# Loading q and k of the third batch in row order, turning two head pairs by TensorE and two by DMA, with the steps ordered anew

## The chip, the cores and the metric

The kernel runs on one core of one Trainium2 chip. The metric is the device time of one execution in microseconds (us). Most executions of one kernel agree within about 1%; an execution whose time is over 1.5% above the fastest of the same kernel is called slow here and is left out of comparisons. The medians quoted are those of all runs of a kernel, the ratios those of its fast runs. The profile of a kernel is one execution; its span (first to last instruction) is 1.7 us shorter than the time of the same execution.

## The reference, cut to what matters

```python
# q, k, v: [4 batches, 8 heads, 768, 64] f32;  window 128, 4 sink tokens
scores = (q @ k.T) / sqrt(64)               # keep: 0 <= i - j < 128, or j < 4
a      = softmax(where(keep, scores, -1e9))
x      = (a @ v) as [4, 768, 512]           # heads side by side
# ---- gated block
h      = gelu_tanh(x @ w_in)                # [4, 768, 1024]
u, v_  = h[..., :512], h[..., 512:]
v_n    = (v_ - mean) / sqrt(var + 1e-6) * g_ln
v_s    = einsum('ts,bsd->btd', w_sg, v_n) + b_sg      # mixes the 768 positions: "spatial"
out    = x + (u * v_s) @ w_out
```

## The kernel before

The kernel is one list of steps, run in the order written. `NAME.b.p` is a step on batch b; each engine takes its own instructions from the list in order. The steps that the argument needs:

- `LQ`, `LK`, `LV`: loads of q, k, v, issued by GpSimd; they are cast to bf16 on the way.
- `TQ`/`TK`, then `EQ`/`EK`: transposes of a head pair on TensorE, and the copy out of PSUM (by ScalarE `A` or VectorE `D`). Where a DMA turns the pair, there is only `EQ`/`EK`, issued by SyncE.
- `KS`, `SK`: the four sink keys of all head pairs of a batch, and their scores. `QK`, `EX`, `MK`, `AV`: scores, exponent, mask (`D` VectorE, `P` GpSimd), product with v.
- `RS`: 1/sigma, a power on GpSimd. `NM`, `Z`: negated mean over sigma, and the normalised v. `SP`: the spatial matmuls. `GT`, `GM`: gate. `OU`, `RA`, `ST`: output matmuls, residual, store. `WT`, `WE`: transposes of w_sg and their copies. `HM.n`: n dummy matmuls.

```python
STEPS = """
... XT.0.3 VSM.1 MV.0.0 XE.0.3.A LV.1.3 VSM.3 VSM.2 MV.0.1 GV.0.0 LG WT.2
... BN.0.2 RS.0.1 WT.4 GU.0.1 TQ.1.1
TQ.1.0 EQ.1.1.A MU.0.2 LQ.2.0 WE.4 EQ.1.0.A NM.0.1 RS.0.2 WE.0 Z.0.3.A ...
... EQ.2.0.D SP.0.0.1 EX.1.3.0 LK.2.0 ...
"""                                     # cut: 655 steps in all
DT = (3,)                               # batches whose q and k are turned by DMA
# ...
qn  = Ring("qn", 4, [128, NT, 2, Dh], BF16)      # row order, one head pair each
kn  = Ring("kn", 4, [128, NT, 2, Dh], BF16)
q16 = Ring("q16", 2, [128, 4, NT, Dh], BF16)     # four heads each
# ...
def load(ring, src, b, i):              # one DMA for four heads, 1536 bytes in a row
    n = 2 if b == 0 else 4
    hs = slice(n * i, n * i + n)
    dst = ring.get((b, n * i // 4))[:, n * i % 4:n * i % 4 + n].rearrange("p h t d -> p h (t d)")
    return nc.gpsimd.dma_start(out=dst, in_=src[b, hs].rearrange("h (p t) d -> p h (t d)", p=128))

def rows(ring, src, b, p):              # row order: one DMA for each head, 256 bytes in a row
    t = ring.new((b, p))
    return [nc.gpsimd.dma_start(out=t[:, :, hl, :], in_=src[b, 2 * p + hl].rearrange("(t p) d -> p t d", p=128))
            for hl in range(2)][-1]

def LQ(b, i):
    if (b, i) == (0, 0):
        return first("q", q)
    return rows(qn, q, b, i) if b in DT else load(q16, q, b, i)
# ...
def transposes(name, ring, b, p):       # 12 transposes of half width
    # ...
    for t in range(NT):
        for hl in range(2):
            nc.tensor.transpose(ps[64 * hl:64 * hl + 64, t, :], src[:, 2 * (p % 2) + hl, t, :], iden)

def turned(dst, name, src, b, p, e):
    if b in DT:
        return nc.sync.dma_start_transpose(out=dst.new((b, p))..., in_=src[b, p]...)
    copy(e, ...)                        # PSUM to SBUF
# ...
def RS(b, jj):
    r = rs[b][:, part(jj)]
    nc.gpsimd.tensor_tensor(r, r, neg_half[:, part(jj)], op=ALU.pow)
```

The softmax here doesn't subtract the row's maximum and nothing guards it: scores larger than these inputs give would overflow.

Of the kernel before, what the change touches and what calls it, by code (L numbers as in the profile page):

```python
# [16 lines left out]
ZERO IDEN LQ.0.0 LK.0.0 LQ.0.1 FILL LK.0.1 LC MASK VSK LV.0.0 MASK0 CQ.0.0.D LQ.0.2 HM.7 TQ.0.0 CK.0.0.D EQ.0.0.A  # L17
LK.0.2 TK.0.0 LV.0.1 EK.0.0.A TQ.0.1 QK.0.0.2 KS.0.0 LQ.0.3 EQ.0.1.D QK.0.0.1 EX.0.0.2 SK.0.0 LK.0.3 VSM.0 TK.0.1
LV.0.2 EK.0.1.D SX.0.0 QK.0.0.0 MK.0.0.2.P EX.0.0.1 HM.1 TQ.0.2 KS.0.1 LV.0.3 EX.0.0.0 QK.0.1.2 EQ.0.2.D SK.0.1
MK.0.0.1.P TK.0.2 EX.0.1.2 QK.0.1.1 EK.0.2.D SX.0.1 QK.0.1.0 LW.0 AV.0.0.1 EX.0.1.1 MK.0.0.0 LW.1 KS.0.2 EX.0.1.0 HM.1  # L20
AV.0.0.0 NR.0.0.1 QK.0.2.2 SK.0.2 MK.0.1.1.P NR.0.0.0 EX.0.2.2 TQ.0.3 TK.0.3 SX.0.2 QK.0.2.1 LWS MK.0.1.0 EQ.0.3.A
QK.0.2.0 EK.0.3.D AV.0.1.0 EX.0.2.1 MK.0.2.2.P NR.0.1.0 EX.0.2.0 LWO QK.0.3.1 MK.0.2.1.D XT.0.0 EX.0.3.1 KS.0.3 LQ.1.0
QK.0.3.0 MK.0.2.0 SK.0.3 AV.0.2.1 XE.0.0.A LK.1.0 MK.0.1.2.D AV.0.2.0 NR.0.2.1 SX.0.3 MK.0.3.1.P QK.0.3.2 AV.0.1.1
EX.0.3.0 NR.0.2.0 LV.1.0 NR.0.1.1 EX.0.3.2 MK.0.3.0 LV.1.1 HM.4 XT.0.2 MK.0.3.2.D XE.0.2.A AV.0.3.0 LQ.1.1 AV.0.3.1
NR.0.3.0 LK.1.1 NR.0.3.1 XT.0.1 LV.1.2 XE.0.1.D XT.0.3 VSM.1 MV.0.0 XE.0.3.A LV.1.3 VSM.3 VSM.2 MV.0.1 GV.0.0 LG WT.2
WT.3 WE.2 WT.5 GV.0.1 MV.0.2 WE.3 BN.0.0 MU.0.0 GV.0.2 WE.5 BN.0.1 WT.0 GU.0.0 MU.0.1 BN.0.2 RS.0.1 WT.4 GU.0.1 TQ.1.1
TQ.1.0 EQ.1.1.A MU.0.2 LQ.2.0 WE.4 EQ.1.0.A NM.0.1 RS.0.2 WE.0 Z.0.3.A MU.0.3 Z.0.0.D Z.0.1.A NM.0.2 Z.0.4.D Z.0.2.A
TK.1.0 Z.0.5.D WT.1 GU.0.3 EK.1.0.D SP.0.1.0 GU.0.2 WE.1 SP.0.1.2 GT.0.1.0 GM.0.1.0.P QK.1.0.1 GT.0.1.2 QK.1.0.0
TQ.1.2 EX.1.0.1 GM.0.1.2.D TQ.1.3 EQ.1.2.D SP.0.1.3 SP.0.0.2 GT.0.1.3 EQ.1.3.A MK.1.0.1.D TK.1.3 EX.1.0.0 GM.0.1.3.D
TK.1.2 GT.0.0.2 QK.1.0.2 EK.1.2.A SP.0.1.1 EK.1.3.D GM.0.0.2.P EX.1.0.2 QK.1.2.2 MK.1.0.0 SP.0.0.3 EX.1.2.2 MK.1.0.2.D  # L30
GT.0.1.1 QK.1.2.0 QK.1.3.0 GT.0.0.3 EX.1.2.0 TQ.2.0 GM.0.1.1.P TK.1.1 EQ.2.0.D SP.0.0.1 EX.1.3.0 LK.2.0 MK.1.2.0
LV.2.0 EK.1.1.A QK.1.2.1 GM.0.0.3.D QK.1.3.2 OU.0.5 EX.1.2.1 GT.0.0.1 LV.2.1 KS.1.0 OU.0.3 EX.1.3.2 RA.0.5 MK.1.2.1.P
SK.1.0 RA.0.3 ST.0.5 QK.1.3.1 SX.1.0 LQ.2.1 QK.1.1.2 MK.1.3.2.D TQ.2.1 ST.0.3 AV.1.0.1 MK.1.3.0 LK.2.1 EQ.2.1.A
AV.1.0.0 MK.1.2.2.D LV.2.2 AV.1.2.0 NR.1.0.1 EX.1.3.1 AV.1.2.1 NR.1.0.0 GM.0.0.1.P TK.2.1 EX.1.1.2 QK.1.1.0 NR.1.2.1
TK.2.0 MK.1.3.1.P EK.2.1.A QK.1.1.1 NR.1.2.0 EX.1.1.0 LV.2.3 MK.1.1.2.D AV.1.3.1 EX.1.1.1 MK.1.1.0 QK.2.1.2 LQ.3.0
AV.1.3.0 NR.1.3.1 EX.2.1.2 OU.0.4 NR.1.3.0 EK.2.0.A MK.1.1.1.P QK.2.1.1 RA.0.4 QK.2.1.0 EX.2.1.1 XT.1.3 LK.3.0 XT.1.1
ST.0.4 XE.1.3.D AV.1.1.0 EX.2.1.0 TQ.2.3 XE.1.1.D AV.1.1.1 NR.1.1.0 LV.3.0 EQ.2.3.A QK.2.0.2 MK.2.1.0 QK.2.0.1 TQ.2.2
EX.2.0.2 LQ.3.1 NR.1.1.1 TK.2.3 EQ.2.2.A TK.2.2 EK.2.3.D XT.1.2 EK.2.2.A LK.3.1 XT.1.0 XE.1.2.D QK.2.0.0 EX.2.0.1
SP.0.0.0 KS.2.0 LV.3.1 EX.2.0.0 XE.1.0.D SK.2.0 GT.0.0.0 MV.1.0 LQ.3.2 SX.2.0 MK.2.0.0 GM.0.0.0.D EQ.3.0 MK.2.0.1.D
OU.0.1 MK.2.0.2.P GV.1.0 AV.2.0.0 RA.0.1 MK.2.1.2.P MV.1.1 MK.2.1.1.P ST.0.1 EK.3.0 BN.1.0 MV.1.2 GV.1.1 BN.1.1  # L40
# [12 lines left out]
QK.3.3.1 AV.3.0.1 NR.3.1.1 AV.3.0.0 Z.2.5.D NR.3.0.1 SP.2.0.1 EX.3.3.1 MK.3.3.2.D QK.3.2.2 NR.3.0.0 MK.3.3.1.P
QK.3.2.1 SP.2.0.3 EX.3.2.2 GT.2.0.1 EX.3.2.1 MK.3.2.2.P AV.3.3.1 GT.2.0.3 QK.3.2.0 NR.3.3.1 MK.3.2.1.P SP.2.0.0
EX.3.2.0 GM.2.0.3.P AV.3.2.1 GT.2.0.0 QK.3.3.0 GM.2.0.1.P NR.3.2.1 SP.2.1.3 EX.3.3.0 XD.3.1 GM.2.0.0.D SP.2.0.2
MK.3.2.0 GT.2.1.3 AV.3.2.0 MK.3.3.0 SP.2.1.2 GM.2.1.3.P GT.2.0.2 AV.3.3.0 NR.3.2.0 SP.2.1.1 GM.2.0.2.P NR.3.3.0
SP.2.1.0 GT.2.1.2 XD.3.0 GT.2.1.1 GM.2.1.2.P OU.2.1 GT.2.1.0 GM.2.1.1.P MV.3.2 RA.2.1 GM.2.1.0.P OU.2.3 GV.3.2 ST.2.1
OU.2.2 RA.2.3 OU.2.4 ST.2.3 RA.2.2 MV.3.0 BN.3.2 ST.2.2 MV.3.1 RA.2.4 RS.3.2 GV.3.0 ST.2.4 NM.3.2 BN.3.0 Z.3.5.A
MU.3.0 GV.3.1 Z.3.4.A OU.2.0 BN.3.1 GU.3.0 MU.3.2 RA.2.0 RS.3.1 MU.3.1 GU.3.2 ST.2.0 NM.3.1 OU.2.5 Z.3.0.A Z.3.3.D
Z.3.1.D Z.3.2.A MU.3.3 RA.2.5 GU.3.1 ST.2.5 SP.3.1.1 GU.3.3 SP.3.0.1 GT.3.1.1 GM.3.1.1.P SP.3.0.3 GT.3.0.1 GM.3.0.1.D  # L60
SP.3.1.0 GT.3.0.3 GM.3.0.3.D SP.3.0.2 GT.3.1.0 GM.3.1.0.P SP.3.0.0 GT.3.0.2 GM.3.0.2.D SP.3.1.3 GT.3.0.0 GM.3.0.0.P
SP.3.1.2 GT.3.1.3 GM.3.1.3.P OU.3.1 GT.3.1.2 OU.3.0 GM.3.1.2.D RA.3.1 OU.3.3 RA.3.0 ST.3.1 OU.3.4 ST.3.0 RA.3.3 OU.3.5
ST.3.3 OU.3.2 RA.3.5 RA.3.2 ST.3.5 ST.3.2 RA.3.4 ST.3.4
"""



HOLDS = "LG<LWS"


DT = (3,)


@with_exitstack
def kernel(
# [127 lines left out]
    def LQ(b, i):  # L203
        if (b, i) == (0, 0):
            return first("q", q)
# [96 lines left out]
    def TQ(b, p):  # L302
        transposes("q", q16, b, p)
# [269 lines left out]
```

## Time and profile before

| | before |
|---|---|
| time, median of 3 runs | 164.76 us (163.81 to 166.53, the last one slow) |
| span, mean granted clock | 160.9 us, 0.998 |
| TensorE busy | 147.7 us (92%) |
| GpSimd busy | 88.9 us (55%) |
| first spatial matmul of batch 1, 2, 3, 4 | 39.87, 84.22, 116.02, 143.14 us |

How to read the profile lines: PE is TensorE, PEld its weight loads, DVE VectorE, ACT ScalarE, POOL GpSimd, SP SyncE. L457 is line 457 of that kernel; x6 counts instructions that stand together; `a<-b` is what is written and what is read; a bracket is the idle time of the engine just before, and what ended it. After is a longer file, so the lines have other numbers there and in the experiments: 1/sigma L457 becomes L474, the spatial matmuls L499 become L528, the output matmuls L516 become L544, the half-width transposes L300 become L305, the row loads L199, the loads of v L214 become L217.

The last row of the table is the ruler. TensorE runs the spatial matmuls of each batch at one fixed place in its own order, so the starts of the four groups cut the span into stretches. (The new order moves a few of TensorE's steps from one stretch to the next, so differences of a few tenths mean nothing.) The starts are read from TensorE's timeline (the chain of waits, from which the prediction took 40.03, counts the first of them 0.16 us later). From start to end the five stretches of before are 39.87, 44.35, 31.80, 27.12 and 17.8 us.

### The profile page before, as it was taken

The numbers are of one execution on the slowest core, as the hardware profiler recorded it, in microseconds if no ns is written. First come the engines' busy times: TensorE is split into PE (matmuls) and PEld (weight loads), VectorE is DVE, ScalarE is ACT, GpSimd is POOL, SyncE is SP. The second block draws the span as 40 slices with busy tenths as digits, with TensorE's granted clock in tenths as the row PEclk, the third lists the DMA queues.
The fourth block names the chain that finished last, engine by engine and source line by source line (L and its number), as shares of the span: only waits on it lengthen the run. The fifth ranks groups of instructions, "written<-read, shape, count | busy, mean of one in ns | idle before, by whom it ended". The sixth has DMA issues, their size and how long they took to land.

```text
span 160.9 us, 3798 instructions
## 1 busy us (share of the span) xinstructions
PE 147.7 (92%) x1508; PEld 86.6 (54%) x1521; DVE 132.0 (82%) x305; ACT 100.4 (62%) x117; POOL 88.9 (55%) x119
## 2 busy tenths in 40 slices
PE   4958798999999979999999999999999999999980
PEld 1436465576655657644565664545756644555530
DVE  4579999599899998977999999789978848857761
ACT  3379985569968789985378678545886025770000
POOL 7999993433226999997994860004076721204400
PEclk9999999999999999999999999999999999999999
DMA  4999999999990999999999955710302545030055
GB/s 162 174 163 175 199 213 206 204 212 176 178 116 5 145 251 183 194 155 145 214 235 164 123 121 108 230 65 9 125 0 48 94 124 195 0 132 0 4 198 195
DMA packets 63122, 22.70 MB, mean 141 GB/s; under 512 B 51456, under 2 KB 59904, under 8 KB 63104
## 3 DMA queue, kind: packets, MB, share of 16 engines
q0 software_dynamic: 45600, 11.80, 75.1%
q1 hardware_dynamic: 17504, 10.66, 26.5%
q8 instruction: 12, 0.20, 0.5%
q14 instruction: 6, 0.05, 0.1%
HBM read 24.81 MB, written 6.29 MB: 193 GB/s over the span
## 4 chain that ended last, share of the span: by engine, by line
PE 64%; POOL 17%; DVE 8%; DMA 3%; ACT 3%; issue 2%; DVEq 0%; POOLq 0%
PE mm L499 18%; PE sc L478 13%; PE mm L516 10%; PE sc L436 10%; POOL v_sb L214 5%; PE sc L350 4%; DMA q<-in_q_dram 3%; DVE x_sb L410 3%; POOL qn L196 3%; PE mm L300 3%; DVE P L365 2%; POOL P L369 2%; POOL kn L196 2%; PE mm L390 2%; ACT P L358 2%
## 5 line engine op out<-in xcount | busy, mean ns | idle before, releaser
L358 ACT ACTIVATE P<-sc 128x1024 bf16<-128x1024 f32 (+1 forms) x48 | 43.9, 962 | 7.0 <-PE sc L350 6.5
L499 PE MATMUL mm<-wsgT,z 128*128 128x384 bf16 x192 | 34.4, 327 | 0.0
L509 POOL TENSOR_TENSOR wsg_gated<-gtmp,uT 128x384 bf16<-128x384 bf16 x19 | 17.9, 951 | 22.9 <-DVE gtmp L504 19.5
L499 PEld LDWEIGHTS <-z 128*128 128x128 bf16 x192 | 17.5, 98 | 12.1 <-issue 1.8
L504 DVE SCALAR_TENSOR_TENSOR gtmp<-mm,g_sb,b_bc 128x384 bf16<-128x384 f32 x32 | 19.4, 614 | 5.6 <-PE mm L499 5.5
L440 ACT ACTIVATE vt<-sc 128x1024 f32<-128x1024 f32 x12 | 12.3, 1024 | 17.0 <-PE sc L436 17.0
L478 PE MATMUL sc<-xT,w_in_sb 128*128 128x384 bf16 x128 | 22.4, 326 | 0.1
L516 PE MATMUL mm<-w_out_sb,wsg_gated 128*128 128x512 bf16 x88 | 21.6, 379 | 0.5 <-issue 0.2
L436 PE MATMUL sc<-w_in_sb,xT 128*128 128x512 bf16 x94 | 21.9, 379 | 0.1
L520 DVE TENSOR_TENSOR ot<-mm,x_sb 128x512 f32<-128x512 f32 x24 | 16.2, 689 | 6.3 <-PE mm L516 6.2
L457 POOL TENSOR_TENSOR rs<-rs,neg_half 128x4 f32<-128x4 f32 (+1 forms) x8 | 7.1, 886 | 25.7 <-DVE rs L452 24.9
L365 DVE TENSOR_TENSOR P<-P,mask 128x1024 bf16<-128x1024 bf16 (+1 forms) x32 | 21.1, 685 | 0.0
L214 POOL DMA_DIRECT2D v_sb<-in_v_dram x16 | 16.9, 1059 | 5.3 <-DMA wsg_gated<-in_moe_w_sg_dram 4.1
L410 DVE TENSOR_TENSOR x_sb<-mm,rcp 128x384 bf16<-128x384 f32 x32 | 17.8, 558 | 1.1
L390 PE MATMUL mm<-v_sb,P 128*128 128x65 bf16 x192 | 17.0, 194 | 1.6 <-DVE P L365 0.9
L484 ACT ACTIVATE uT<-sc 128x768 bf16<-128x768 f32 x16 | 12.8, 807 | 8.1 <-PE sc L478 8.1
L449 DVE BATCH_NORM_STATS2 st<-vt 128x6 f32<-128x512 f32 x24 | 16.2, 675 | 1.5 <-ACT vt L440 1.5
L478 PEld LDWEIGHTS <-w_in_sb 128*128 128x128 bf16 x128 | 12.4, 98 | 9.0
L390 PEld LDWEIGHTS <-P 128*128 128x128 bf16 x192 | 14.5, 98 | 4.7 <-DVE P L365 1.6
L396 PE MATMUL mm<-v_sb,P 128*128 128x65 bf16 x160 | 15.7, 194 | 0.6 <-POOL P L373 0.4
L350 PE MATMUL sc<-qT,kT 64*128 64x256 bf16 x192 | 15.5, 264 | 0.7 <-DVE kT L221 0.3
L436 PEld LDWEIGHTS <-xT 128*128 128x128 bf16 x96 | 9.2, 98 | 10.5 <-issue 0.2
(73 smaller groups left out, 227.4 us busy)
## 6 DMA issues: line engine op xcount, KB each, us to landing
out_dram<-ot SPq DMA_DIRECT2D x24, 256.0 KB, 2.3
v_sb<-in_v_dram POOLq DMA_DIRECT2D x16, 192.0 KB, 7.9
q<-in_q_dram POOLq DMA_DIRECT2D x4, 384.0 KB, 13.7
k<-in_k_dram POOLq DMA_DIRECT2D x4, 384.0 KB, 13.1
wsg_gated<-in_moe_w_sg_dram POOLq DMA_DIRECT2D x1, 1152.0 KB, 12.3
w_in_sb<-in_moe_w_in_dram POOLq DMA_DIRECT2D x2, 512.0 KB, 7.6
qn<-in_q_dram POOLq DMA_DIRECT2D x8, 96.0 KB, 7.2
kn<-in_k_dram POOLq DMA_DIRECT2D x8, 96.0 KB, 6.0
```

Source lines behind the costliest of these rows:

```text
L214: return nc.gpsimd.dma_start(out=v_sb[b % len(v_sb)][:, 2 * p:2 * p + 2, :, 0:Dh].rearrange("p h t d -> p (h t) d"), in_=v[b, 2 * p:2 * p ...
L350: nc.tensor.matmul(sc[:, hl, 256 * jl:256 * jl + n], kT[b, p][rows, 128 * j:128 * (j + 1)], qT[b, p][rows, 128 * j:128 * j + n], start=Tru ...
L358: nc.scalar.activation(out=pt[:, :, 0:w], in_=sc_ring[b, p, g][:, :, 0:w], func=AF.Exp, scale=scale)
L365: nc.vector.tensor_mul(pt[:, :, 0:w], pt[:, :, 0:w], m.unsqueeze(1).to_broadcast([128, 2, w]))
L390: nc.tensor.matmul(av[:, il, hl, :], P[b, p, i // 2][:, hl, 256 * (i % 2):256 * (i % 2) + 128], vb[:, h, i, :], start=first, stop=False)
L410: nc.vector.tensor_mul(xs[:, 3 * half:3 * half + 3, 128 * p:128 * (p + 1)].rearrange("p t (h d) -> p t h d", h=2), av[:, :, :, 0:Dh], rcp. ...
L436: nc.tensor.matmul(hp[:, jl, :], xT[b][:, j, c, :], w_in_sb[:, c, d_half:2 * d_half], start=(c == 0), stop=(c == KD - 1))
L478: nc.tensor.matmul(hp[:, n, 0:NH], w_in_sb[:, c, 128 * dc:128 * (dc + 1)], xT[b][:, 3 * hf:3 * hf + 3, c, :], start=(c == 0), stop=(c == K ...
L499: nc.tensor.matmul(ps[:, 0:NH], z[b][:, si, 128 * dc:128 * (dc + 1)], wsgT[:, si, NH * hf:NH * (hf + 1)], start=(si == 0), stop=(si == NT ...
L504: nc.vector.scalar_tensor_tensor(out=gtmp.new((b, hf, dc)), in0=mm_ring["g", b, hf, dc][:, 0:NH], scalar=g_sb[:, dc:dc + 1], in1=b_bc[:, N ...
L509: (nc.vector if e == "D" else nc.gpsimd).tensor_mul(gatedT[:, (2 * b + hf) % 3, dc, :], gtmp[b, hf, dc], uT[b][:, dc, NH * hf:NH * (hf + 1)])
L516: nc.tensor.matmul(ps, gatedT[:, (2 * b + hf) % 3, dc, 128 * tl:128 * (tl + 1)], w_out_sb[:, dc, :], start=(dc == 0), stop=(dc == KU - 1))
```

## The change

Its intent: q and k of the third batch come in row order, as those of the fourth do already. Then two of the four head pairs need no TensorE transpose (a DMA turns them), and the other two are turned in full width, 6 transposes in place of 12. The third batch gets buffers of its own at once, so that its loads no longer wait for transposes of the first two. The last output tiles leave partly in halves, and the whole list of steps is ordered anew.

```diff
-DT = (3,)
+TURN = ('SSSS', 'SSSS', 'RRDD', 'DDDD')      # per batch and head pair: S half width, R rows and TensorE, D rows and DMA
+LAST = (5,)                                  # output tiles of the last batch that leave in halves

 def LQ(b, p):
     ...
-    return rows(qn, q, b, i) if b in DT else load(q16, q, b, i)
+    return load(q16, q, b, p) if TURN[b][p] == "S" else rows(qn, q, b, p)      # LK the same

 def transposes(name, s, r, b, p):
     for t in range(NT):
+        if TURN[b][p] == "R":
+            nc.tensor.transpose(ps[:, t, :], r[b, p][:, t, :, :].rearrange("p h d -> p (h d)"), iden)
+            continue
         for hl in range(2): ...

 def turned(dst, name, src, b, p, e):
-    if b in DT:
+    if TURN[b][p] == "D":
         return nc.sync.dma_start_transpose(...)
+    if TURN[b][p] == "R":
+        return copy(e, ...)                   # contiguous
...                                           # cut: OU, RA, ST in halves (OB, RB, SB); parts MA, UA that no step uses
 STEPS (the piece around the first batch's 1/sigma; the rest is cut, all of it is reordered)
-... BN.0.2 RS.0.1 WT.4 GU.0.1 TQ.1.1 TQ.1.0 EQ.1.1.A MU.0.2 LQ.2.0 WE.4 EQ.1.0.A NM.0.1 RS.0.2 WE.0 ...
+... XT.0.3 LQ.2.0 MV.0.0 VSM.2 XE.0.3.D LK.2.0 VSM.3 MV.0.2 GV.0.0 VSM.1 LV.2.0 LG LQ.2.1 WT.4 WT.1 WE.4 WT.0 GV.0.2
+    WT.2 BN.0.0 LK.2.1 WT.5 MV.0.1 LV.2.1 WE.2 BN.0.2 MU.0.2 GV.0.1 LQ.2.2 MU.0.3 BN.0.1 GU.0.2 LK.2.2 MU.0.0 GU.0.3
+    RS.0.2 WE.1 RS.0.1 NM.0.2 MU.0.1 WE.0 Z.0.4.A ...
```

## The prediction

> **What bounds the kernel now**
>
> I read the page first (busy time, the 40 slices, the chain), then the chain in order of time, GpSimd's timeline, and the transfers by window. The span is 160.9 us; the time before is 164.76 us, so I predict the difference in the span and add it to 164.76.
>
> ```profile
> PE 147.7 (92%) x1508; PEld 86.6 (54%) x1521; DVE 132.0 (82%) x305; ACT 100.4 (62%) x117; POOL 88.9 (55%) x119
> PE   4958798999999979999999999999999999999980
> POOL 7999993433226999997994860004076721204400
> DMA  4999999999990999999999955710302545030055
> PE 64%; POOL 17%; DVE 8%; DMA 3%; ACT 3%; issue 2%; DVEq 0%; POOLq 0%
> ```
>
> TensorE is full from slice 8 to the tail; what it loses lies in the first 30 us and the last 10. So what TensorE no longer does is saved, as long as nothing starves it. The transfers are as full: from slice 1 to 11 (4 to 48 us) the DMA row says 9, slice 12 is 0, then full again to 92 us. GpSimd looks free between 24 and 50 us. It is not free to issue loads, which is the point of this prediction:
>
> ```profile
> 24.62 0.77 POOL L192 DMA_DIRECT2D k<-in_k_dram  x1
> 29.44 1.03 POOL L214 DMA_DIRECT2D v_sb<-in_v_dram  x1 [4.05 <-DMA wsg_gated<-in_moe_w_sg_dram]
> 31.59 1.01 POOL L214 DMA_DIRECT2D v_sb<-in_v_dram  x1 [1.12 <-DMA w_out_sb<-in_moe_w_out_dram]
> 34.99 1.05 POOL L457 TENSOR_TENSOR rs<-rs,neg_half 128x4 f32<-128x4 f32 x1 [2.39 <-DVE rs L452]
> 36.74 0.81 POOL L192 DMA_DIRECT2D q<-in_q_dram  x1 [0.70 <-PE mm L300]
> 37.57 0.73 POOL L457 TENSOR_TENSOR rs<-rs,neg_half 128x2 f32<-128x2 f32 x1
> ```
>
> This is GpSimd's timeline of before (start, duration, what ended the idle time). Two loads of v stood still, with GpSimd idle, until two other loads had landed. Those are the loads eight places earlier in GpSimd's stream: the load at 29.44 waited for the one landed at 28.75, the load at 31.59 for 31.29. The built program says the same: GpSimd's loads take eight completion semaphores in turn, each waiting for its own last user. And L457, the power that makes 1/sigma of the first batch, stands in the same stream. Before, only one load (36.74) stands between its two halves and none has to land late for it.
>
> Everything of the first batch's gating hangs on these two: Z, then the spatial matmuls (L499).
>
> ```profile
> 36.43 2.71 PE sc L478 x16
> 39.13 0.46 PE mm L300 x12
> 39.59 0.44 PE mm L491 x6
> 40.03 1.95 PE mm L499 x12
> 45.37 0.79 PE mm L300 x24
> ```
>
> In the chain of before, TensorE goes from the u matmuls over one transpose of k (12 pieces, 0.46 us) and one of w_sg (6, 0.44) straight into L499 at 40.03, without a gap.
>
> **What the Trainium skill says**
>
> "DMA: Bandwidth & Descriptors", Anatomy of one DMA: the DMA engines do not wait on semaphores; a wait happens on the issuing sequencer before dispatch. The trace agrees: 4.05 and 1.12 us of GpSimd idle. "TensorE: Matmul & The Clock Gate", the table of specifications, gives ScalarE, VectorE and GpSimdE strict FIFO queues; so work behind a waiting load waits too. Both timelines keep program order, and no instruction in them overtakes. The DMA page's Specifications give about 27 GiB/s per engine and line rate only from 512 B. Trace: from 68 to 72 us 4,785 packets of 256 B read ended, 64/4785 = 13.4 ns per packet and engine (19 GB/s); with that taken off, the packets of 1536 B read from 60 to 64 us cost 60 ns (25.6 GB/s). It agrees in kind. The clock-gate page, Part 1, says that about 3.4 us of idleness halves TensorE's clock until it has been busy as long. Trace: 12 transposes took 0.85 us at 5.36 us and 0.53 at 7.05.
>
> **The change part by part**
>
> *TensorE.* Eight half-width turns of the third batch (12 transposes each) go. The chain shows 24 in 0.79 us, 33 ns each[...]: 8 x 0.395 = 3.2 us. Four full-width turns come, 6 each; the w_sg transposes (L491) have that shape, 0.33 us for six: 1.3 us. Net 1.9 us saved, nearly all of it from the two pairs that go to DMA; full width alone saves 0.07 us per turn. Dummy warming matmuls stay 13.
>
> *Copies out of PSUM.* The third batch drops from eight to four, all ScalarE (about 0.80 us each); the new steps move others about. ScalarE in all loses about 4 us, VectorE about 2 (four masks at 0.70 move to GpSimd). Neither bounds.
>
> *GpSimd.* q and k of that batch were 4 loads of 0.78 us; now 16 of 0.84: +10.3 us. Four masks come (+5), one product goes. Busy about 103 us; no bound by itself.
>
> *Transfers.* 2048 packets at 60 ns become 12288 at 13.4 ns: per engine 7.7 becomes 10.3 us, +2.6 us. The idle slice 12 and the end at 92 us could hide that.
>
> *The last tile in halves.* In the new order the halved tile (5) is not the last to leave: tile 4 is added and stored after it, whole. I expect 0 within 0.2 us.
>
> *The steps anew.* Before, the third batch's loads reused the ring of the first two and waited for transposes (36.74, and the next at 50.51). Now they have free buffers, and the new steps put them at once behind the second batch's. Counting GpSimd's stream in the built program of after from load 0: second batch 14 to 21, then q2.0 22-23, k2.0 24-25, v 26, q2.1 27-28, k2.1 29-30, v 31, q2.2 32-33, k2.2 34-35, and only then the two L457. So L457 of the first batch sits behind fourteen more loads, and load 35 can't be issued before load 27 has landed.
>
> When does 27 land? The loads up to 21 are the same in both kernels and nearly in the same order, and the DMA was full all that time, so they land as before: load 14 at 34.4 us, 21 at 46.7. Then four row loads (48 packets per engine x 13.4 ns = 0.64 us each) and one v (1.4 us) and 27 itself: 46.7 + 2.6 + 1.4 + 0.6 = 51.3 us. Load 35 is issued just after (0.3 us of semaphore, 0.84 of issue), with GpSimd's own pace giving about the same: 53.0. Then L457 0.73 and 1.05: 53.7 and 54.8, where before they ended at 36.0 and 38.3.
>
> What waits: VectorE has the negated mean of the last two tiles, and behind it the w_sg copy WE.0 that frees a PSUM buffer, so TensorE stops even before the last turns of q, at about 38.5. From 53.7 VectorE has two negated means (0.15 each), two w_sg copies (0.55) and three Z at 0.54, done at 56.8 (the second mean can't go before 54.8). ScalarE has three Z and one gelu at 0.75 to 0.8 each from 53.9, then the copy of q1.1 (0.80), which frees the PSUM buffer of the first L499: about 58. So L499 starts at 58 instead of 40: +18 us of nearly empty TensorE. A cold clock after that costs about 1.2 us (a window of 3.4 us, part of it on short turns).
>
> After 58 TensorE had 116.3 us to do (40.0 to 156.3), of which 1.9 are saved; its gaps in that stretch sum to some 1.5 us, and as all loads are now early I give half back. Sum: +18 + 1.2 - 1.9 - 0.8 = +16.5. 164.8 + 16.5 = 181; I say 180.
>
> **The rivals**
>
> 1. *The loads don't hold GpSimd.* Had the waits slack in after, or landed the loads sooner, the change would show its intent: -1.9 of transposes, up to -1.5 of gaps, giving 161.5 to 163: a gain of 1 to 2%. For it: someone ordered the steps so, which suggests a schedule in which the loads issue freely. Against: the two waits above, and a DMA that is full from 4 to 48 us, so bytes cannot come sooner. Only a small chance.
>
> 2. *Only part of the stall reaches the end.* If TensorE found work in its stream ahead of the first L499, or the DMA turned out faster on 256 B rows, the delay would be 8 to 12 us: 170 to 175. The order of TensorE's instructions has nothing there but one turn of q, one of k and one of w_sg (1.3 us), so I give it little.
>
> 3. *Late row loads starve the fourth batch.* +2.6 us of transfer and waits of its loads on the DMA turns of the third (shared buffers) could cost 1 to 3 us at QK of the fourth. Against: before, the last load landed at 92.9 us, and the second half of batch four is first used at about 114. With a stall of 18 us compute is later still. No effect.
>
> 4. *The copies and the lighter ScalarE* matter only where those engines release TensorE, under 1 us.
>
> **Range and chances**
>
> With the stall (about nine in ten) the result lies between 174 and 186: the landing of load 27 is good to about 2 us, the path from L457 to the first L499 to 2, the reordered rest to 2. Rivals 1 and 2 take the rest. Predicted 180 us, range 172 to 186. Faster by over 2%: 0.03; within 2%: 0.07; slower by over 2%: 0.90.
>
> **What would show it**
>
> - GpSimd's timeline: a chain of qn and kn loads from about 34 to 53 us, each idle before it with a DMA named, then L457 at about 53 instead of 35. If L457 runs before 40, the main step is wrong.
> - TensorE's slices: two to four near-zero digits between 38 and 58 us; first L499 near 58. Right size if the gap is 15 to 19 us.
> - The chain of waits: GpSimd's qn and kn issue lines and DMA in place of TensorE between 35 and 55 us.
> - The transposes of q and k: 192 at half width and 24 at full, TensorE's busy time down by about 2 to 3 us.
> - The DMA row: slice 12 no longer empty, loads ending relative to compute much earlier.
> - The tail: as before, from the last L516 to the end 4.6 us.
>
> I am wrong if loads land quickly enough that no wait on GpSimd shows, or if an unseen second stall in the middle makes it over 186.

## The result

After took 185.45 us (median of 4 runs: 185.34, 185.44, 185.46, and one slow of 188.68) beside 164.28 of before (162.67 to 166.53, the last one slow). Ratios here are the mean time of one kernel's fast runs over that of the other's in the same rounds, so they are not quite the ratio of the medians quoted: 1.132, 95% interval 1.121 to 1.144. The profiled execution has a span of 183.7 us, 22.8 more than before.

| | before | after | difference |
|---|---|---|---|
| span | 160.9 | 183.7 | +22.8 |
| start to spatial group of batch 1 | 39.87 | 56.94 | +17.1 |
| batch 1 to batch 2 | 44.35 | 49.66 | +5.3 |
| batch 2 to batch 3 | 31.80 | 32.84 | +1.0 |
| batch 3 to batch 4 | 27.12 | 26.49 | -0.6 |
| batch 4 to the end | 17.8 | 17.8 | 0.0 |

The page of after, the rows that answer to those of the prediction (busy times; 40 slices of 4.6 us; the chain):

```profile
PE 151.2 (82%) x1440; PEld 88.0 (48%) x1453; DVE 131.8 (72%) x304; ACT 96.6 (53%) x112; POOL 102.5 (56%) x138
...
PE   5759679990037999999595999999998999999990
...
POOL 8998952355999565499678134852215641032720
PEclk9987999996555999999999699999999999999999
DMA  5999999999999933499999970945400065113044
...
PE 53%; DMA 21%; POOL 14%; ACT 4%; issue 2%; DVE 2%; DVEq 0%; POOLq 0%; ACTq 0%
```

TensorE has two slices of 0 and one of 3 (41 to 55 us), and a second, shallower dip (the 5 9 5 between 87 and 101 us). Its granted clock is 0.5 to 0.6 in the first hole and just behind it, and 0.6 once more behind the second dip. The chain now holds 21% of DMA where it held 3%.

GpSimd's timeline of after around the first hole (start, duration, line, tile, and in brackets the idle time before it and what ended that):

```profile
34.94 0.82 POOL L199 DMA_DIRECT2D qn<-in_q_dram  x1 [2.10 <-DMA q<-in_q_dram]
38.51 0.82 POOL L199 DMA_DIRECT2D kn<-in_k_dram  x1 [0.70 <-DMA v_sb<-in_v_dram]
...
50.56 1.68 POOL L199 DMA_DIRECT2D kn<-in_k_dram  x2
52.20 1.78 POOL L474 TENSOR_TENSOR rs<-rs,neg_half 128x2 f32<-128x2 f32 x2
```

Row loads stand one behind the other, each of the first idle until an older load has landed, and the power that makes 1/sigma (L474, which was L457) comes at 52.2 us in place of 35.0. TensorE's timeline of after shows what that stops:

```profile
53.72 0.85 PE L305 MATMUL mm<-iden,q 128*64 128x128 bf16 x12 [12.68 <-DVE wsgT L523]
...
56.94 2.08 PE L528 MATMUL mm<-wsgT,z 128*128 128x384 bf16 x6 [0.98 <-ACT qT L222]
```

12.68 us of TensorE wait on a VectorE copy (`WE`) that stands behind the negated mean, which stands behind the power. The spatial matmuls (L528) start at 56.94, and six of them take 2.08 us at half clock, where warm ones take 1.1.

The second dip, in the same two views. First GpSimd, in which L376 is a mask of the third batch:

```profile
89.03 1.65 POOL L199 DMA_DIRECT2D kn<-in_k_dram  x2 [1.51 <-DMA v_sb<-in_v_dram]
90.68 0.66 POOL L376 TENSOR_SCALAR_AFFINE_SELECT P<-P 128x512 bf16<-128x512 bf16 x1
...
96.42 0.82 POOL L199 DMA_DIRECT2D kn<-in_k_dram  x1 [1.08 <-DMA qn<-in_q_dram]
...
99.00 0.65 POOL L376 TENSOR_SCALAR_AFFINE_SELECT P<-P 128x512 bf16<-128x512 bf16 x1
...
99.99 1.70 POOL L474 TENSOR_TENSOR rs<-rs,neg_half 128x4 f32<-128x4 f32 x2
```

Then TensorE, which needs the masked P for the product with v:

```profile
91.39 0.20 PE L397 MATMUL mm<-v_sb,P 128*128 128x65 bf16 x1 [2.11 <-POOL P L376]
...
99.71 0.20 PE L397 MATMUL mm<-v_sb,P 128*128 128x65 bf16 x1 [2.12 <-POOL P L376]
...
100.24 5.75 PE L495 MATMUL sc<-xT,w_in_sb 128*128 128x384 bf16 x24
```

Now it is the fourth batch's row loads that stand in front of two masks of the third and of the second batch's 1/sigma. The table by window (busy time of TensorE, its weight loads, VectorE, ScalarE and GpSimd with instruction counts, then the granted clock; the two columns of DMA at the end are not used here) shows the size of both holes:

```profile
40.00:50.00 10.00, 1.04 (x16) 0.55 (x15) 0.00 (x0) 0.00 (x0) 7.03 (x9) 0.66 2.21 163
50.00:60.00 10.00, 5.30 (x52) 3.36 (x51) 6.77 (x12) 5.59 (x7) 9.39 (x12) 0.50 1.93 132
...
90.00:100.00 10.00, 6.23 (x54) 3.53 (x55) 7.05 (x18) 3.54 (x4) 8.17 (x12) 1.00 1.70 192
100.00:110.00 10.00, 10.00 (x68) 5.28 (x65) 4.71 (x12) 6.76 (x8) 3.14 (x5) 0.83 1.53 112
```

Between 40 and 50 us VectorE and ScalarE did nothing at all, and TensorE 1.04 us: everything waits for the one power on GpSimd, which itself was busy for 7 us issuing loads.

The second dip has a cold clock of its own: for 3.41 us from 101.1 the granted clock was 0.5 (mean 0.83 between 100 and 110), and the 24 u matmuls (L495) in it took 5.75 us, where 32 took 5.36 at full clock. That is about 1.7 us of the 5.3 (an estimate from these two lines).

### The profile page after: what moved, and what is told of

The parts are those of the page before. It is cut to its first block, busy times and chain, and to the rows that moved or that the text cites. A ratio compares the mean times of both kernels' runs of the same rounds, so it can differ in the third digit from the quotient of the medians.

```text
span 183.7 us, 3700 instructions
## 1 busy us (share of the span) xinstructions
PE 151.2 (82%) x1440; PEld 88.0 (48%) x1453; DVE 131.8 (72%) x304; ACT 96.6 (53%) x112; POOL 102.5 (56%) x138
## 4 chain that ended last, share of the span: by engine, by line
PE 53%; DMA 21%; POOL 14%; ACT 4%; issue 2%; DVE 2%; DVEq 0%; POOLq 0%; ACTq 0%
PE mm L528 18%; DMA v_sb<-in_v_dram 12%; PE mm L544 9%; DMA w_out_sb<-in_moe_w_out_dram 9%; PE sc L495 9%; PE sc L443 7%; PE sc L357 4%; POOL v_sb L217 3%; POOL kn L199 3%; PE mm L397 2%; PE mm L403 1%; POOL q L195 1%; ACT z L483 1%; PE mm L305 1%; POOL k L195 1%
## 5 line engine op out<-in xcount | busy, mean ns | idle before, releaser
L528 PE MATMUL mm<-wsgT,z 128*128 128x384 bf16 x192 | 35.2, 333 | 1.0 <-ACT qT L222 1.0
L538 POOL TENSOR_TENSOR wsg_gated<-gtmp,uT 128x384 bf16<-128x384 bf16 x18 | 16.9, 945 | 19.2 <-DVE gtmp L533 19.1
L528 PEld LDWEIGHTS <-z 128*128 128x128 bf16 x192 | 17.9, 99 | 14.3 <-issue 2.9
L495 PE MATMUL sc<-xT,w_in_sb 128*128 128x384 bf16 x128 | 23.8, 343 | 0.0
L376 POOL TENSOR_SCALAR_AFFINE_SELECT P<-P 128x512 bf16<-128x512 bf16 x20 | 13.7, 685 | 16.5 <-ACT P L365 15.8
L544 PE MATMUL mm<-w_out_sb,wsg_gated 128*128 128x512 bf16 (+1 forms) x93 | 22.2, 370 | 0.4
L397 PE MATMUL mm<-v_sb,P 128*128 128x65 bf16 x192 | 17.8, 196 | 5.3 <-POOL P L376 4.2
L457 ACT ACTIVATE vt<-sc 128x1024 f32<-128x1024 f32 x12 | 12.3, 1023 | 17.5 <-PE sc L443 17.5
L372 DVE TENSOR_TENSOR P<-P,mask 128x1024 bf16<-128x1024 bf16 (+1 forms) x28 | 20.1, 731 | 0.5 <-ACT P L365 0.5
L552 DVE TENSOR_TENSOR ot<-mm,x_sb 128x512 f32<-128x512 f32 (+1 forms) x25 | 15.9, 663 | 4.2 <-PE mm L544 4.2
L357 PE MATMUL sc<-qT,kT 64*128 64x256 bf16 x192 | 16.8, 272 | 2.3 <-ACT P L365 1.7
L417 DVE TENSOR_TENSOR x_sb<-mm,rcp 128x384 bf16<-128x384 f32 x32 | 17.8, 557 | 1.1
L495 PEld LDWEIGHTS <-w_in_sb 128*128 128x128 bf16 x128 | 13.1, 102 | 10.0 <-issue 1.7
L199 POOL DMA_DIRECT2D qn<-in_q_dram x16 | 13.4, 847 | 7.3 <-DMA k<-in_k_dram 2.2
L305 PE MATMUL mm<-iden,q 128*64 128x128 bf16 x96 | 4.9, 248 | 14.7 <-DVE wsgT L523 12.7
## 6 DMA issues: line engine op xcount, KB each, us to landing
q<-in_q_dram POOLq DMA_DIRECT2D x2, 384.0 KB, 17.1
```

What stands on the lines that cost most here:

```text
L357: nc.tensor.matmul(sc[:, hl, 256 * jl:256 * jl + n], kT[b, p][rows, 128 * j:128 * (j + 1)], qT[b, p][rows, 128 * j:128 * j + n], start=Tru ...
L372: nc.vector.tensor_mul(pt[:, :, 0:w], pt[:, :, 0:w], m.unsqueeze(1).to_broadcast([128, 2, w]))
L397: nc.tensor.matmul(av[:, il, hl, :], P[b, p, i // 2][:, hl, 256 * (i % 2):256 * (i % 2) + 128], vb[:, h, i, :], start=first, stop=False)
L417: nc.vector.tensor_mul(xs[:, 3 * half:3 * half + 3, 128 * p:128 * (p + 1)].rearrange("p t (h d) -> p t h d", h=2), av[:, :, :, 0:Dh], rcp. ...
L495: nc.tensor.matmul(hp[:, n, 0:NH], w_in_sb[:, c, 128 * dc:128 * (dc + 1)], xT[b][:, 3 * hf:3 * hf + 3, c, :], start=(c == 0), stop=(c == K ...
L528: nc.tensor.matmul(ps[:, 0:NH], z[b][:, si, 128 * dc:128 * (dc + 1)], wsgT[:, si, NH * hf:NH * (hf + 1)], start=(si == 0), stop=(si == NT ...
```

## The experiments

The theory before them: row loads on GpSimd are what costs, first by standing in front of the first batch's 1/sigma (+17.1 us), then by standing in front of the third batch's masks (+5.3 us). The rivals: the new order as a whole is at fault and the row loads only happen to lie in it; the DMA turns are what costs; the cold clock costs more than was thought. Thirteen kernels ran. Times of before on the same chips: 163.07 (with half_issues, rs_first, spread, old_order), 163.96 (spread2, old_order_r, tail), 163.98 (masks_first, warm, tail4, spread2_r), 163.63 (spread3_r, masks_warm). All gave a correct result but spread2_r; half_issues puts heads in wrong places and passed all the same; that this is because q and k have a scale of 0.1, which makes the attention weights nearly even, is likely but was not tested.

### half_issues: half as many row loads for the same packets

```diff
 def rows(ring, src, b, p):
-    return [nc.gpsimd.dma_start(out=t[:, :, hl, :], in_=src[b, 2 * p + hl].rearrange("(t p) d -> p t d", p=128)) for hl in range(2)][-1]
+    return nc.gpsimd.dma_start(out=t.rearrange("p t h d -> p (t h) d"),
+                               in_=src[b, 2 * p:2 * p + 2].rearrange("h (t p) d -> p (h t) d", p=128))   # heads in wrong places
```

> Wrong result on purpose: each row-order load fetches both heads of a pair in one DMA instead of two, with the heads in the wrong places; the bytes, the packets and their sizes stay as in the changed kernel, only the number of load instructions and of their waits is halved for the third and fourth batch. Theory (GpSimd runs in order and a load waits for the landing of the load eight before): the first 1/sigma power now stands behind eight loads fewer; it should run at 47 to 50 us instead of 52.2, the first spatial matmul at 52 to 54 instead of 56.9, the second stall shrink by 2 to 5 us, and the time fall from 185 to 175 to 180 us. Rival (the bytes in 256-byte rows arrive too slowly): same packets, so no change, 183 to 187 us.

175.94 us, ratio 1.082 (1.072 to 1.091). TensorE's first wait and the first spatial group:

```profile
49.23 0.85 PE L305 MATMUL mm<-iden,q 128*64 128x128 bf16 x12 [9.36 <-DVE wsgT L523]
...
52.45 2.08 PE L528 MATMUL mm<-wsgT,z 128*128 128x384 bf16 x6 [0.98 <-ACT qT L222]
```

The wait shrank from 12.68 to 9.36 us and the group starts 4.5 us earlier; the second starts at 97.07, 44.6 us later, as in before (44.35). Bytes and packets are the same, so these 4.5 us and the second stall belong to the number of load instructions. From the first of the third batch's loads to the power it is 12.5 us in place of 17.3 on GpSimd's timeline: 3.7 us less of issuing and 1.1 less of waiting. What stays of the first stall, 8.1 us of issuing eight loads and 4.4 of waiting until older loads had landed, this run does not take apart.

### rs_first: the third batch's loads behind the first 1/sigma

```diff
-XT.0.3 LQ.2.0 MV.0.0 VSM.2 XE.0.3.D LK.2.0 ... LV.2.0 LG LQ.2.1 ... LK.2.1 ... LV.2.1 ... LQ.2.2 ... LK.2.2 ... RS.0.2 WE.1 RS.0.1
+XT.0.3 MV.0.0 VSM.2 XE.0.3.D ... RS.0.2 WE.1 RS.0.1 LQ.2.0 LK.2.0 LV.2.0 LQ.2.1 LK.2.1 LV.2.1 LQ.2.2 LK.2.2
```

> The changed kernel with one edit: the eight load steps (fourteen DMAs) of the third batch that stood ahead of the first batch's 1/sigma power stand right behind it. Theory (anything behind waiting loads waits): the power runs at 35 to 38 us and the first spatial matmul starts at 40 to 41 us as before; but the first gating product on GpSimd stays behind all twenty loads, at 56 to 59 us, and with three buffers for its input VectorE and then TensorE stop at about 46; so the stall shrinks only from about 15 to 10 or 11 us: 179 to 182 us. Rival (the position of that power alone is the cause): the whole first stall goes, 167 to 170 us. Rival (data late): no change, 185.

181.32 us, ratio 1.111 (1.103 to 1.120), in the expected range, though the first group starts at 43.81 us and not at 40 to 41: its second power ran at 39.62 (37.57 in before), having waited for VectorE. The first stall is gone, and another has come in its place:

```profile
43.81 1.14 PE L528 MATMUL mm<-wsgT,z 128*128 128x384 bf16 x6 [0.71 <-ACT qT L222]
...
60.16 2.08 PE L528 MATMUL mm<-wsgT,z 128*128 128x384 bf16 x6 [6.65 <-DVE gtmp L533]
```

GpSimd's timeline of the same kernel tells why: the gate products (L538), which give VectorE its three gtmp buffers back, stand behind the last of those loads.

```profile
57.41 1.11 POOL L217 DMA_DIRECT2D v_sb<-in_v_dram  x1
58.44 1.88 POOL L538 TENSOR_TENSOR wsg_gated<-gtmp,uT 128x384 bf16<-128x384 bf16 x2
```

The first spatial group came 13 us earlier, and 4 us of it reached the end. A block of some 20 load issues stops whatever stands behind it on GpSimd, wherever the block is put.

### masks_first: the fourth batch's loads behind the masks

```diff
-... MK.2.1.1.D LV.3.1 XE.1.1.A ... ST.0.3 LQ.3.2 ... LK.3.2 ... MK.2.0.1.P ... LV.3.2 ... LQ.3.3 ... LK.3.3 ... LV.3.3 GV.1.1 MK.2.1.2.P ... RS.1.2
+... MK.2.1.1.D XE.1.1.A ... ST.0.3 ... MK.2.0.1.P LV.3.1 LQ.3.2 LK.3.2 ... GV.1.1 MK.2.1.2.P ... RS.1.2 LV.3.2 LQ.3.3 LK.3.3 LV.3.3
```

> Change of one thing in after: seven load steps of the fourth batch (one v, the third q pair, the third k pair; then v, the last q pair, the last k pair, v) move behind the masks and the second batch's 1/sigma powers that they stood in front of on GpSimd; the first stall is left as it is. Theory (the second stall is the fourth batch's loads standing ahead of third-batch masks): the spatial group of the second batch starts 44.5 to 46.5 us after that of the first (49.7 in after, 44.35 in before), no TensorE wait over 1.5 us on a GpSimd mask between 80 and 105 us, and the time falls from 185.4 to 179 to 182 us. Rival (the second stall comes from the DMA turns or from the cold clock after the first stall): 184 to 187 us with the group distance still above 48.

180.28 us, ratio 1.101 (1.095 to 1.108). The two groups are now 43.95 us apart (57.20 and 101.15), where after had 49.66 and before 44.35. TensorE's waits (line waited for, total us, times, longest), after first, then masks_first:

```profile
PE mm L397 <- POOL P L376: 4.2, 2, 2.1
```

```profile
PE mm L397 <- POOL P L376: 0.4, 1, 0.4
```

So the second stall is the fourth batch's loads in front of the masks, and it cost 5 us of the time. The rival (DMA turns or the cold clock behind the first stall make it) falls: both are in masks_first too. The second cold stretch of after is gone with its waits; the granted clock of masks_first is 1.0 from 62.8 us almost to the end.

### warm and masks_warm: the cold clock measured

```diff
-... NM.0.1 TQ.1.1 Z.0.0.D ...
+... NM.0.1 HM.55 TQ.1.1 Z.0.0.D ...        # 55 dummy matmuls in the hole; warm: in after, masks_warm: in masks_first
```

> After with 55 dummy matmuls put into the first stall of TensorE (in front of the turn of the second q pair of the second batch), nothing else changed. Theory (the stall also leaves a cold clock behind that costs about 1 us on the path): granted clock near 1.0 between 50 and 60 us (0.50 in after), the first six spatial matmuls in 1.1 us instead of 2.08, and 183.3 to 184.8 us. Rival (the slow matmuls after the stall lie beside VectorE's and ScalarE's own backlog, so the clock costs nothing): 185.0 to 186.0 us.

The total is inconclusive: 182.0 and 183.3 us in the two runs marked fast, 185.1 to 186.2 in the four marked slow, and a recorded ratio of 1.130 (1.122 to 1.138), not to be told from 1.132. That ratio must hold slow runs; the two fast ones alone would give about 1.12. The profile is clearer. The window from 50 to 60 us of warm, and two of its TensorE lines:

```profile
50.00:60.00 10.00, 8.45 (x89) 4.55 (x87) 6.73 (x12) 6.29 (x8) 9.54 (x12) 1.00 1.86 122
```

```profile
57.15 1.13 PE L528 MATMUL mm<-wsgT,z 128*128 128x384 bf16 x6 [1.42 <-ACT qT L222]
...
71.50 2.75 PE L544 MATMUL mm<-w_out_sb,wsg_gated 128*128 128x512 bf16 x11
```

The clock is 1.00 where it was 0.50. From the first spatial matmul to the first output matmuls (L544) it is 71.50 - 57.15 = 14.35 us; in after it is 72.47 - 56.94 = 15.53. The cold clock cost 1.2 us. The rest of what warm's profile gained (its span is 180.2) lies behind that, in the second stall, which was 2.6 us shorter in this execution. Some 1.7 us of it is the second cold stretch, which did not come here (granted clock 1.00 between 100 and 110 us, where after has 0.83); why the rest is shorter, this run does not tell.

> Both single changes to after together: the fourth batch's loads behind the masks, and 55 dummy matmuls in the first stall. So the cold clock after the first stall is measured without the second one, against masks_first of 180.3 us. If the prediction's 1.2 us for the clock was right: 178.5 to 179.7 us in the fast state. If the two fast runs of the run warm (2.8 us below after) show its size: 177 to 178.4. If their gain came from the second stall only: 179.8 to 180.8.

180.94 us, ratio 1.107 (1.101 to 1.112): no gain over masks_first, and inconclusive for the clock. In its profile GpSimd came to the power 1.4 us later than in masks_first (53.89 in place of 52.45), since loads in front of it landed later, and TensorE stood still twice between the dummies and the group (1.73 and 1.92 us), after which the clock was at half again:

```profile
58.63 1.92 PE L528 MATMUL mm<-wsgT,z 128*128 128x384 bf16 x6 [1.92 <-ACT qT L222]
```

From the first group to the second it took 42.92 us in place of 43.95, so 1.0 us came back and 1.4 was lost ahead of it. The dummies did not delay those loads: one of v had landed at 40.23 us in place of 38.46 already, and the first dummy ran at 41.19. The execution differed before it came to the edit.

### old_order and old_order_r: the steps of before with row loads

```diff
 # before's list; each load of q, k of the third batch becomes two row loads in its place
-... MU.0.2 LQ.2.0 WE.4 ... EX.1.3.0 LK.2.0 ... SX.1.0 LQ.2.1 ... MK.1.3.0 LK.2.1 ...
+... MU.0.2 LQ.2.0 LQ.2.1 WE.4 ... EX.1.3.0 LK.2.0 LK.2.1 ... SX.1.0 LQ.2.2 LQ.2.3 ... MK.1.3.0 LK.2.2 LK.2.3 ...
 TURN for the third batch: 'RRDD' in old_order, 'RRRR' (all four by TensorE) in old_order_r; no halves
```

> The row-order loads and the turns (two pairs by TensorE in full width, two by DMA) in the steps of the kernel before: each load of four heads replaced in place by four row loads, the turns of two pairs left to SyncE; no halves in the tail. Theory: TensorE saves 1.9 us, but four loads stand where one stood; the one between the two halves of the first 1/sigma power delays the second half from 37.6 to about 42 us (first spatial matmul group ends about 4 us late), and the later ones add 2.6 us three times on GpSimd in the stretch 50 to 75 us where its chain ended last: 168 to 175 us. Rival (only the new steps are at fault, the forms are a gain): 161 to 164 us.

187.32 us, ratio 1.148 (1.141 to 1.155): a clear miss, and the most useful one. With the order of before, the row loads and DMA turns together cost even more than in after. The delay of 4 us that was expected ahead of the first group did not come (it starts at 39.86); the loss lies behind it. Its two stalls, on TensorE, and the VectorE line that the second one waits for:

```profile
71.23 0.24 PE L397 MATMUL mm<-v_sb,P 128*128 128x65 bf16 x1 [7.94 <-POOL P L376]
...
91.45 0.69 PE L343 MATMUL mm<-qT,ks_sink 128*32 128x512 bf16 x2 [9.19 <-DVE ks_sink L330]
```

```profile
91.01 0.46 DVE L330 TENSOR_TENSOR ks_sink<-kT,halfsel 128x8 bf16<-128x8 bf16 x2 [10.07 <-DMA kT<-kn]
```

The first is the known one, a mask behind loads. The second is new: the sink keys need k of all four pairs, and the turn of the last k pair was issued at 82.14 us and landed at 90.99. Its row loads had landed by 72.20. In SyncE's own stream it stands behind a store and three other turns: the store, whose addition on VectorE ran at 75.62 behind the first stall, went out at 76.34, and the turns from 76.86 on. So this stall is in part a consequence of the first.

> As old_order (the steps of the kernel before), but all four pairs of the third batch are turned by TensorE from row-order loads, none by DMA. Its trace showed two stalls of TensorE: 7.9 us at 71 us for a mask behind row loads on GpSimd, and 9.2 us at 91 us for the sink keys, which waited for the DMA turn of k of the last pair. Theory (two separate causes, the issue of row loads on GpSimd and the DMA turn's latency): the second stall goes or falls under 3 us, the first stays at 6 to 9 us, and the time falls from 187 to 176 to 181 us. Rival (both stalls come from the row loads alone): the second stall stays, 185 to 189 us.

176.40 us, ratio 1.075 (1.069 to 1.080). The wait on the turn is gone, the one on the mask stays:

```profile
68.43 0.24 PE L397 MATMUL mm<-v_sb,P 128*128 128x65 bf16 x1 [7.21 <-POOL P L376]
```

So there are two costs, of which the second can be taken away alone: load issues on GpSimd, and the delay of a DMA turn (its place in SyncE's order and its own time). In after no wait on a DMA turn shows; that its stalls left the turns time enough is likely, but not tested.

### spread, spread2, spread2_r and spread3_r: can an order hide the row loads?

```diff
 # after's list with the loads of batches three and four taken out and put back one or two at a time behind GpSimd's own work
+spread2: RS.0.1 LQ.2.0 | Z.0.5.A LK.2.1 | EQ.1.1.A LQ.2.1 | GM.0.0.2.P LK.2.0 | MK.1.0.2.P LQ.2.2 LK.2.2 | GM.0.1.0.P LQ.2.3
+         MK.1.3.1.P LK.2.3 LV.2.0 | MK.1.1.1.P LV.2.1 LV.2.2 LV.2.3 | SP.0.0.3 LQ.3.0 LK.3.0 LV.3.0 | MK.2.0.1.P LQ.3.1 LK.3.1
+         MK.2.1.2.P LV.3.1 LQ.3.2 LK.3.2 | RS.1.2 LV.3.2 LQ.3.3 | GM.1.1.0.P LK.3.3 | MK.2.3.1.P LV.3.3;  EK.2.3 behind ST.0.3
 # spread: the same idea, each v load beside its q and k, so the last k row load comes later
 # spread2_r: spread2 with TURN 'RRRR' and TQ/TK in front of EQ/EK;  spread3_r: TK.2.3 EK.2.3 moved ahead of OU.0.0
```

> The changed kernel with the loads of the third and fourth batch spread over GpSimd's stream: each is put where the load eight before has landed by then, behind the powers, masks and products that TensorE waits for; two DMA turns are put behind two stores. Nothing else moves. Theory: both stalls go, the first spatial matmul is at 40 to 42 us, no wait of TensorE over 2 us between 30 and 90 us; 163 to 170 us, as my hand placement can leave small waits. Rival (the new forms or the transfers themselves cost it, not the placement): 178 us or more.

175.45 us, ratio 1.074 (1.068 to 1.081): half of the loss is gone (the first spatial group starts at 42.77), but not to the 163 to 170 that I expected. The wait on a DMA turn that old_order has came here too, on VectorE, and TensorE's sink scores (L343) waited 6.36 us for that:

```profile
78.56 0.17 DVE L330 TENSOR_TENSOR ks_sink<-kT,halfsel 128x8 bf16<-128x8 bf16 x1 [6.58 <-DMA kT<-kn]
```

The turn of the last k pair was issued at 71.63 us and landed at 78.54.

> As spread, but all sixteen row loads of q and k of the third batch go ahead of that batch's loads of v, and the last turn of k directly behind two stores. The trace of spread showed what its place had missed: the sink keys of the third batch (one VectorE step for all four pairs) waited 6.6 us for the DMA turn of k of the last pair, which landed at 78.5 us. Theory (that wait is the load's place plus 6 to 7 us of the turn): it falls under 2 us, and the time from 175.5 to 166 to 170 us. Rival (the turn itself is slow wherever it stands): no change, 174 to 177 us.

171.38 us, ratio 1.046 (1.040 to 1.052), a little above the expected range. With the last k pair loaded earlier the wait is short:

```profile
74.57 0.17 DVE L330 TENSOR_TENSOR ks_sink<-kT,halfsel 128x8 bf16<-128x8 bf16 x1 [1.78 <-DMA kT<-kn]
```

The turn itself took 9.0 us from issue to landing here (65.54 to 74.54).

> As the run spread2, with all four pairs of the third batch turned by TensorE in full width, none by DMA. Theory (in spread2 the wait for the last k pair's DMA turn cost up to 1.8 us, and the two DMA turns save TensorE about 1.3 us of turns): the wait of the sink-key copy on a DMA turn is gone and the time is within 1.5 us of spread2's 171.4, so 170 to 172.5. Rival (DMA turns slow the loads beside them and cost more than shows as a wait): 166 to 169. Other rival (ScalarE's four more copies hold up the scores): 173 to 175.

A wrong result (relative error 0.69), at 168.13 us. The step TK.2.3 used one more of the four PSUM buffers, so that SK.2.0 overwrote output tile 1 of the first batch before RA.0.1 had added it. The list decides what lies in a buffer, and playing the list through, buffer by buffer, gives this one clash and no other; in spread2 and spread3_r there is none. The repair moves the two steps ahead of the output tiles:

> The run spread2_r gave a wrong result: with one more PSUM buffer in use around the last turn of k, the sink scores of the third batch took the buffer of an output tile of the first before it had been added. Here that turn and its copy stand five steps earlier, ahead of the three output tiles, and nothing else differs. Theory (the wrong result came of that alone, and its time was sound): correct, and 167 to 169 us, so that the two DMA turns of spread2 cost about 3 us more than they saved TensorE. Rival (the lost buffer had hidden a wait): correct, 170 to 172 us.

Correct, 169.43 us, ratio 1.036 (1.031 to 1.042): between the ranges of the two theories. Against spread2 (1.046) that is 1% less without DMA turns, but the two intervals overlap (1.040 to 1.052 and 1.031 to 1.042) and two steps stand elsewhere, so that the turns cost more than the TensorE transposes they save is likely here and not shown. In old_order it is shown. This is the best order with row loads that I found, and it is still 3.6% slower than before. By the ruler (41.50, 89.35, 123.43, 149.92 us) it loses 1.6 us ahead of the first group, 3.5 us between the first and the second, 1.8 us after that. No TensorE wait over 1.0 us stands in the middle one; the order was not tuned around the new places of the loads, and whether tuning would win it back stays open. The new list with the old four-head loads was not run, so how much of the 3.6% is the order and how much the row loads stays open too.

### tail and tail4: the halves alone

```diff
 # before's list and loads; only the end differs
-OU.3.4 ST.3.0 RA.3.3 OU.3.5 ST.3.3 OU.3.2 RA.3.5 RA.3.2 ST.3.5 ST.3.2 RA.3.4 ST.3.4
+OU.3.4 ST.3.0 RA.3.3 OU.3.5 ST.3.3 OU.3.2 RA.3.4 OB.3.2 ST.3.4 RA.3.5 ST.3.5 RA.3.2 ST.3.2 RB.3.2 SB.3.2
+LAST = (2,)
+ot = Ring("ot", 4, ...)                     # tail4 only; 3 in tail and before
```

> The kernel before with only its tail changed: the tile that TensorE finishes last (2) leaves in halves, and the tile that VectorE added last though it was ready (4) is added before it. The third batch is loaded and turned as before. The last addition then covers half a tile (about 0.42 us, as the halves of tile 5 in the changed kernel) and ends about 0.8 us earlier: ratio 0.993 to 0.998 to the kernel before. If the store's landing alone sets the end, nothing changes: 0.998 to 1.002.

163.49 us, ratio 0.996 (0.991 to 1.001): inconclusive. VectorE waited for a store to free one of three output buffers:

```profile
157.14 0.69 DVE L552 TENSOR_TENSOR ot<-mm,x_sb 128x512 f32<-128x512 f32 x1 [0.82 <-DMA out_dram<-ot]
```

> Before with its last output tile in halves and last in the stream, as in the run tail, and with four output buffers in place of three. Theory (in the run tail VectorE waited 0.8 us for a store to give back one of three buffers): no wait of VectorE on a store in the last 10 us, and a ratio to before of 0.990 to 0.996. Rival (the last store's own time from issue to landing sets the end, whatever the halves): 0.996 to 1.002.

162.69 us, ratio 0.994 (0.988 to 1.001). The wait is gone, as the last additions of tail4 show:

```profile
157.02 0.76 DVE L552 TENSOR_TENSOR ot<-mm,x_sb 128x256 f32<-128x256 f32 x2 [0.18 <-PE mm L544]
```

A gain of half a per cent is likely, but the interval holds 1.0, so it is not shown. It has the lowest median.

## Why the prediction was right or wrong

The direction and the main mechanism were right. The size was too small: predicted was a rise of 15.2 us (180 over 164.76, 9.3%), measured a ratio of 1.132, which is 21.8 us on the same base and puts the result at or just past the upper end of the range (185.45 us as measured, 186.5 on the prediction's base). Of the 6.6 us that are missing, 1.3 had been taken off the sum (181.3) without a reason ("I say 180"); nearly all the rest is the second stall. Term by term:

- **The stall of the first batch, predicted +18.** Measured +17.1 on the ruler. The chain of its parts held: the power was predicted at 53.0 and ran at 52.2; the first spatial matmul was predicted at 58 and started at 56.94 (TensorE stopped at 41.0, not at 38.5, which changes nothing in the sum). The steps between (eight places for loads, landing of load 27 predicted at 51.3) were about 1 us pessimistic: it landed at 49.98, so at the end GpSimd's own pace of 0.83 us for each row load was the limit, which the working had put at the same size. The row loads landed 0.62 us apart (0.64 in the working). half_issues shows that 4.5 us of the stall go with the number of load instructions, rs_first that they must stand ahead of the power to delay it.
- **The cold clock, predicted +1.2.** Measured 1.2 behind the first stall, by the same stretch in one execution each of after and warm; masks_warm could not confirm it in the total. The second cold stretch, about 1.7 us, has no term; it came with the second stall. It also came without the idleness of 3.4 us that the prediction took as the condition: no wait before it was longer than 2.12 us, but in the 3.41 us before it TensorE's records are busy for 42% only.
- **Turns saved, predicted -1.9, and gaps, predicted -0.8.** The half-width transposes fell to 192 and the full-width ones are 24, as predicted. TensorE's busy time rose, though, from 147.7 to 151.2 us, where a fall of 2 to 3 was predicted: slow instructions at half clock count as busy (the u matmuls 23.8 us in place of 22.4, the spatial ones 35.2 in place of 34.4), which explains a part and was not thought of. The net of both terms can be read where no stall is in the way: masks_first takes 43.95 us from the first group to the second, 0.4 less than before, with 1.2 us or more of cold clock in it. So about 1.6 us was saved there, an estimate, since the order in this stretch is new as well.
- **The step that failed: rival 3, "Late row loads starve the fourth batch", with its verdict "No effect", and with it the half of the gaps "given back" because "all loads are now early".** The working looked at whether the fourth batch's data come in time, and they do. It did not look at what stands behind those loads on GpSimd. Two masks of the third batch and the second batch's 1/sigma do, and the stretch between the first and the second group grew by 5.3 us; against the 43.95 of masks_first it is 5.7. With the seven steps moved, the kernel takes 180.28 us; its ratio of 1.101 gives 181.4 on the prediction's base, which is the prediction's sum of 181.3. So the prediction had a sum without its second stall. Its last sentence names "an unseen second stall in the middle" as what would make it wrong, but no term stood for it. The error was to follow GpSimd's stream instruction by instruction only up to the first power; the same count, made for the loads of the fourth batch and the masks marked `P`, would have shown it.
- **The copies (rival 4) and the halves.** As predicted: no VectorE or ScalarE bound shows (ScalarE lost 3.8 us where about 4 was expected, VectorE 0.2 where about 2), and the tail from the last group to the end is 17.8 us in both.
- **What neither the prediction nor after's waits showed:** a DMA turn took 2.7 to 9.4 us to land (the 71 turns of q and k whose landing the 15 traces hold), and the sink keys wait for all four. In after no wait on it shows; in spread and old_order it showed as waits of 6 to 9 us. To take turns off TensorE by DMA cost 7% in the old order (old_order against old_order_r); in the best order found, a gain from it is not shown, and a loss of 1% is likely (spread2 against spread3_r).

Of the gain of 1 to 2% that the change was meant for (rival 1 of the prediction) nothing is left in any order tried: each head's row load costs GpSimd as much issue time (0.82 us) as a load of four heads did (0.73 to 0.81), and GpSimd is in the path of every batch through masks, gate products and 1/sigma.

## What to carry to other kernels

Before adding loads to an engine that also computes, write out that engine's own stream, and for each computing instruction count the loads in front of it, the time of an issue, and the load that must land first; do it for the whole stream, not only for the first stall found. Judge a load by the number of instructions it takes as well as by its bytes. And if an experiment takes one wait away, look for the next one in the same place before the gain is believed: here a DMA's own delay lay behind the queue.

## What the Trainium skill lacked or had wrong

- "DMA: Bandwidth & Descriptors", section "Why a DMA increments its semaphore by 16 and not by 1", advises one semaphore for each slot in flight; no page says what it costs when the slots run out. Here GpSimd's loads used eight in turn, and the ninth waits for the first: 4.05 and 1.12 us of idle GpSimd in before, and the waits of 0.4 to 2.1 us of after's load queue, behind which TensorE stood still for 12.68 us.
- The same page, section "Anatomy of one DMA": it puts the dispatch at about 50 ns and the making of descriptors at "small, variable"; its section "Latency and other measured facts" has about 1 us to the first byte on this path, which is nearer. In these traces a row load of 96 KB (768 packets of 256 B) holds GpSimd for 0.82 us and a load of v for 1.01 us; twelve more such issues, placed ahead of GpSimd's own work, are the main cost of this change.
- "Anatomy of one DMA" fits about 2.0 us plus bytes/436e3 for one DMA, an estimate of 2.2 us for a row load (96 KB written). From issue to landing it was 3.1 us at the least in after, 7.1 in the median for row loads of q and 8.5 for loads of v, most of them with the DMA row at 9; the fit is no guide in a full queue.
- "DMA: Bandwidth & Descriptors", section "DMA Transpose (X-bar)", lists constraints, and other places of the skill a bandwidth, but no delay. From issue to landing, one 128x768 bf16 turn of q or k took 2.7 us (after, issued at 113.4 us, where the DMA row shows 0) to 9.4 us (half_issues). Only some turns have a landing in a trace; of the six of k in after it is two, with 4.2 and 8.2 us.
- No page says how busy TensorE must be to keep its full clock (it would belong to "TensorE: Matmul & The Clock Gate"). The granted clock of these traces changes on a grid of 3.41 us. Of the 680 such windows at full clock in the 15 traces, the 32 in which TensorE's records are busy for under 48% were all followed by half clock, the 634 with over 57% by none, the 14 between by either (worked out from the matmul records, of which some can be missing).
